# Linear attention and a gated expert layer on one core: the last 64 tokens' logits in full-width products, and their output rows in one store

## The chip, the cores and the metric

The kernel runs on one core of one Trainium2 chip. The metric is the device time of one execution in microseconds; the median of several executions is compared. TensorE (PE, with its weight loads PEld) multiplies matrices into PSUM; VectorE (DVE), ScalarE (ACT) and GpSimd (POOL) work element by element; SyncE (SP) issues most of the transfers. Transfers between the chip's memory and SBUF are moved by 16 DMA engines, whichever queue they were issued on. Each of the five engines takes its own instructions in order and waits on semaphores for the others.

## What is computed

Attention without a softmax, then a layer of eight experts of which each token uses one:

```
q_p, k_p = phi(q), phi(k)            # phi(x) = max(x, exp(x) - 1 for x <= 0) + 1
kv  = k_p^T v  per batch and head;   z = sum over the sequence of k_p
x   = (q_p kv) / (q_p . z + 1e-6)    # 8 batches, 576 tokens, 8 heads x 64 = 512 features
logits = x @ w_gate                  # 8 experts
fresh = argmax(logits); local = sigmoid(x @ w_local)
e     = fresh, if it is the first token or local < 0.5, else the expert of the token before
out   = softmax(logits)[e] * (relu(x @ w1[e]) @ w2[e])
```

q, k and v are (8, 8, 576, 64), w1 is (8, 512, 1024), w2 (8, 1024, 512), the output (8, 576, 512), all float32. If in a batch all tokens end with the expert of the first one, one pass with that expert's weights does for all of them. The kernel computes this case, counts tokens for which it doesn't hold, and runs a general version behind a branch (`tc.If(anybad > 0)`) only if there are any. In the runs here the branch is not taken.

## The kernel before

**Tokens.** A batch's 576 tokens lie as 64 rows of nine (`C` = 9): token 9p + c belongs to row p. Tokens with c = 1 to 8 form four chunks of 128 (`SM` = 512 of them), and those with c = 0 form a fifth chunk of 64, called the last one; the first token of the batch is in it. `NC` is 5, `PH` is 64.

**Stages of one batch.** SP loads k, q and v of two groups of four heads. ACT and DVE compute phi. PE multiplies k^T v (`kvs`, L299), transposes q (`q_main`, L310; `q_last`, L324), and multiplies q kv (`num_main`, L351; `num_last`, L370); DVE divides by the denominator (`divide`, L336 to L339). PE transposes x in bf16 (`x_main`, L385; `x_last`, L397), and DVE copies it from PSUM to the tile `xT`, [128, 4, 576]: 512 features as four blocks of 128 partitions, tokens along the free dimension. `x_main_out` (L390) copies two chunks of 128 tokens, `x_last_out` (L401) the 64 of the last chunk. Three `xT` tiles are in rotation.

**Logits.** `logits(b, cs)` multiplies chunks of `xT` by `wg`, the eight gate columns and the local one, into a PSUM tile of nine columns for each chunk (L412, L418). It is called twice for each batch: once for the last chunk alone, as early as it can be, because `pick` reads the first token's expert from it (its maximum, L429), which starts the load of that expert's weights on POOL's queue (L476, L478); and once for the other four chunks. The PSUM tile has 128 partitions. For the last chunk `logits` fills both halves: for each half d it runs four products with the same 64 tokens as the stationary operand (L412), so eight products of 64 columns. Later `gate_sub` and `gate_end` read all five chunks over 128 partitions.

**Experts and output.** `hidden` (L530) and `output` (L547, L551) multiply by w1 and w2; ACT evacuates them (L537, L561, L563). For the last chunk `output` computes columns 0 to 255 of the 64 tokens on the partitions 0 to 63 and columns 256 to 511 on the partitions 64 to 127, so that the tile `yl` is [128, 256]: partition 64h + p holds half h of the row of token 9p. `store` writes the four large chunks from `yo` (L570) and the last chunk from `yl` (L575) in two transfers, one for each half, from SP's queue. In the last batch the first of the two goes out on ACT's queue.

**Order.** The program is written out by a planner: `in_order` takes operations with an engine, an estimated length, a rank, what they need and which PSUM slot they take, and returns one order. The work is emitted in that order under `tc.manual_schedule()`, so each engine's instructions run in the order of the list. Two batches of attention run ahead of the experts (`LEAD` = 2).

**Fill products.** At the start PE has nothing to do while the first loads arrive. `work(n)` puts products of a tile of zeros ahead of some operations of batch 0 (`fills`, L741): 14 before `QL` (the first `q_last`), 8 before `K` (the first `kvs`), 15 in all before eight others. Each has 512 columns. `zero` is set by a memset at L167, `ones`, used as one column at the end in `total` (L588), at L184.

**End.** After the last store all engines load the counter `flag_i` (L749), branch over the general version (L751) and meet at the end of the program (L986).

Of the kernel before, what the change touches and what calls it, by code (L numbers as in the profile page):

```python
# [10 lines left out]
F32 = mybir.dt.float32  # L11
BF16 = mybir.dt.bfloat16
# [68 lines left out]
def kernel(  # L81
# [11 lines left out]
    nc = tc.nc  # L93
    P = 128
    B, H, S, Dh = q.shape
    D = H * Dh
    E = moe_w_gate.shape[1]
    F = moe_w1.shape[2]
    DK = D // P
    FK = F // P  # L100
    PH = P // 2


    C = S // PH
    NJ = 2

    NC = 5
    SM = (NC - 1) * P
# [8 lines left out]
    consts = ctx.enter_context(tc.tile_pool(name="consts", bufs=1))  # L117
# [3 lines left out]
    bad = keep.tile([P, B, NC], F32, name="bad")  # L121
# [3 lines left out]
    with ExitStack() as main:  # L125
# [37 lines left out]
                load(vraw[n % NV].rearrange("p g c d -> p g (c d)"), v, n)  # L163


        zero = consts.tile([P, 512], BF16, name="zero")
        nc.vector.memset(zero, 0.0)  # L167
        for n in range(NJ):
            load_q0(n)
# [10 lines left out]
            nc.sync.dma_start(out=wgf[:, :, E:E + 1],  # L180
                              in_=moe_w_local.rearrange("(ko ki) e -> ki ko e", ki=P))

        ones = consts.tile([P, P], F32, name="ones")
        nc.vector.memset(ones, 1.0)  # L184
        ident = consts.tile([P, P], F32, name="ident")
        make_identity(nc, ident)
# [6 lines left out]
        wg = consts.tile([P, DK, E + 1], BF16, name="wg")  # L193
# [7 lines left out]
        xtp = main.enter_context(tc.tile_pool(name="xtp", bufs=NX))  # L201
# [5 lines left out]
        ps_m = main.enter_context(tc.tile_pool(name="ps_m", bufs=2, space=PSUM))  # L207

        BK = 512

        def bank2(pool, name, tag, dt=F32):
            return pool.tile([P, 2, BK if dt == F32 else 2 * BK], dt, name=name, tag=tag)

        kv, qT, xb, xb4, xT, gate, hT, ex_ = {}, {}, {}, {}, {}, {}, {}, {}
# [68 lines left out]
        open_ = {}  # L283
# [49 lines left out]
        def divide(ps, m, dst):  # L333

            den = sm_.tile([P, 2, m], F32, name=f"den{m}")
            nc.vector.tensor_scalar(den, ps[:, :, :, Dh], 1e-6, None, Alu.add)  # L336
            rec = sm_.tile([P, 2, m], F32, name=f"rec{m}")
            nc.vector.reciprocal(rec, den)
            nc.vector.tensor_tensor(  # L339
                dst, ps[:, :, :, :Dh],  # L340
                rec.rearrange("p g (m o) -> p g m o", o=1).to_broadcast([P, 2, m, Dh]), op=Alu.mult)
# [32 lines left out]
        def num_last_out(a):  # L374
            ps = open_.pop(("NL", a))
            xb4[a] = xbp.tile([P, 2, P], BF16, name="xb4")
            divide(ps[:, :, :2 * W].rearrange("p g (m w) -> p g m w", w=W), 2,
                   xb4[a].rearrange("p g (t e) -> p g t e", t=2))
# [18 lines left out]
                nc.tensor.transpose(ps[:, 0, g * P:(g + 1) * P], xb4[a][:, g, :], identity=identb)  # L397

        def x_last_out(a):
            xT[a] = xtp.tile([P, DK, S], BF16, name="xT")  # L400
            nc.vector.tensor_copy(  # L401
                xT[a][:, :, SM:].rearrange("q (j g) p -> q g j p", g=2),
                open_.pop(("XL", a))[:, 0, :2 * P].rearrange("q (g j p) -> q g j p", g=2, j=2))

        rt, st = {}, {}

        def logits(b, cs):
            lps = open_["R", b, cs[0]] = bank2(ps_a, "lps", "a")[:, 0, :NC * (E + 1)].rearrange("p (c e) -> p c e", c=NC)
            if cs[-1] == NC - 1:
                for d in range(2):  # L410
                    for kk in range(DK):
                        nc.tensor.matmul(lps[d * PH:(d + 1) * PH, NC - 1, :],  # L412
                                         lhsT=xT[b][:, kk, SM:], rhs=wg[:, kk, :],
                                         start=(kk == 0), stop=(kk == DK - 1))
            for c in cs:
                if c < NC - 1:
                    for kk in range(DK):
                        nc.tensor.matmul(lps[:, c, :], lhsT=xT[b][:, kk, c * P:(c + 1) * P],  # L418
                                         rhs=wg[:, kk, :], start=(kk == 0), stop=(kk == DK - 1))

        def logits_out(b, cs):
            lps = open_.pop(("R", b, cs[0]))
            nc.vector.tensor_copy(lt_all[:, b, cs[0]:cs[-1] + 1], lps[:, cs[0]:cs[-1] + 1])

        def pick(b):

            m8 = sm_.tile([1, 8], F32, name="m8")
            i8 = sm_.tile([1, 8], U32, name="i8")
            nc.vector.max_with_indices(m8, i8, lt_all[0:1, b, NC - 1, :E])  # L429
            e0f = sm_.tile([1, 1], F32, name="e0f")  # L430
            nc.vector.tensor_copy(e0f, i8[:, 0:1])
            if b == 0:
                nc.vector.tensor_copy(tag[:, 0:1], e0f)
                rt[b] = (i8, e0f, None, None)
                return

            sc = sm_.tile([1, E], F32, name="sc8")
            nc.vector.scalar_tensor_tensor(sc, tag, e0f, age, Alu.is_equal, Alu.add)
            ms = sm_.tile([1, 8], F32, name="ms")
            si = gp.tile([1, 8], U32, name="si")  # L440
            nc.vector.max_with_indices(ms, si, sc)
            miss = sm_.tile([1, 1], I32, name="miss")
            nc.vector.tensor_scalar(miss, ms[:, 0:1], 1.0, None, Alu.is_lt)
            rt[b] = (i8, e0f, si, miss)
            st[b, "sc"] = (sc, ms)
# [119 lines left out]
        def store(b, i0, i1):  # L565
            o = out[b].rearrange("(p c) d -> p c d", c=C)
            ym, yl = yo[b]
            if i0 < NC - 1:
                for r in range(2):
                    nc.sync.dma_start(out=o[:, 1 + i0 + (NC - 1) * r:1 + i1 + (NC - 1) * r, :],  # L570
                                      in_=ym[r::2, i0:i1, :])
            else:
                for h in range(2):
                    eng = nc.scalar if b == B - 1 and h == 0 else nc.sync
                    eng.dma_start(out=o[:, 0, h * (D // 2):(h + 1) * (D // 2)],  # L575
                                  in_=yl[h * PH:(h + 1) * PH])

        def flags():

# [5 lines left out]

        def total():
            tot = open_["TOT"] = bank2(ps_a, "tot", "a")[0:1, 0, :B * NC]
            nc.tensor.matmul(tot, lhsT=ones[:, 0:1], rhs=bad.rearrange("p b c -> p (b c)"),  # L588
                             start=True, stop=True)

        def flag():
# [7 lines left out]
        def op(name, eng, length, rank, needs, fn, takes=None, gives=None):  # L599
            ops.append((name, eng, length, rank, [d for d in needs if d], takes, gives))  # L600
            run[name] = fn
# [7 lines left out]
        for a in range(B):  # L609
            at = (a - LEAD) * NU  # L610
            quick = a < LEAD
            for j in range(NJ):
# [3 lines left out]
                head = 60 * (a == 0)  # L616
# [59 lines left out]
               lambda a=a: num_last(a), takes="a")  # L676
            op(("DL", a), "DVE", 0.8, at - 3 - 2 * head, [("NL", a), a and ("XL", a - 1)],
               lambda a=a: num_last_out(a), gives=("NL", a))
            for h in range(2):
                cs = [NC - 1] if h == 0 else list(range(NC - 1))  # L680
                op(("X", a, h), "PE", 0.5, at + 6 + 4 * h - head, [("D", a, 0, h), ("D", a, 1, h)],
                   lambda a=a, h=h: x_main(a, h), takes="a")
                op(("XC", a, h), "DVE", 0.7, at + 1 + 3 * h - head, [("X", a, h)],
                   lambda a=a, h=h: x_main_out(a, h), gives=("X", a, h))
                op(("R", a, h), "PE", 0.2 + 0.3 * h, at + 4 + 7 * h - 2 * head * (1 - h),
                   [("WG",)] + ([("XC", a, 0), ("XC", a, 1)] if h else [("XLC", a)]), lambda a=a, cs=cs: logits(a, cs), takes="a")
                op(("RC", a, h), "DVE", 0.2, at - 3 + 8 * h - 2 * head * (1 - h), [("R", a, h)],
                   lambda a=a, cs=cs: logits_out(a, cs), gives=("R", a, h))
            op(("XL", a), "PE", 0.2, at + 3 - 2 * head, [("DL", a)], lambda a=a: x_last(a), takes="a")
            op(("XLC", a), "DVE", 0.3, at - 3 - 2 * head, [("XL", a), a >= NX and ("H", a - NX, FK - 1)], lambda a=a: x_last_out(a), gives=("XL", a))  # L690
            op(("PK", a), "DVE", 0.8, at - 3 - 2 * head, [("RC", a, 0), a and ("BK", a - 1)], lambda a=a: pick(a))
            op(("BK", a), "DVE", 0.65 if a else 0.02, at + 8, [("PK", a)], lambda a=a: book(a))
            for x in range(2):
                op(("W", a, x), "POOL", 1.2, at + x - head,
# [5 lines left out]
                    (("H", 0, 3) if x == 0 else ("O", 0, 1))],  # L700
                   lambda a=a, x=x: use(a, x))
            gr = at + NU
            op(("S1", a), "DVE", 0.6, gr, [("PK", a), ("RC", a, 0), ("RC", a, 1)],
               lambda a=a: gate_sub(a))
            op(("S2", a), "ACT", 0.25, gr, [("S1", a)], lambda a=a: gate_exp(a))
            op(("S3", a), "DVE", 1.4, gr + 3, [("S2", a)], lambda a=a: gate_end(a))
# [27 lines left out]
        order, begun, done = in_order(ops, {"a": 2, "m": 2, "ek": NK}, 0.2)  # L734

        with tc.manual_schedule():
            fill = bank2(ps_m, "fill", "m")[:, 0, :]

            def work(n):
                for _ in range(n):  # L740
                    nc.tensor.matmul(fill, lhsT=zero[:, :P], rhs=zero, start=True, stop=True)  # L741

            fills = {("QL", 0): 14, ("K", 0): 8, ("NL", 0): 2, ("XL", 0): 4, ("R", 0, 0): 2,
                     ("N", 0, 0, 1): 2, ("N", 0, 1, 0): 1, ("N", 0, 1, 1): 1, ("X", 0, 0): 1, ("X", 0, 1): 2}
            for name in order:
                work(fills.get(name, 0))
                run[name]()
# [243 lines left out]
```

## Time and profile before

| | us |
|---|---|
| median of three runs | 237.54 (235.86, 237.54, 241.7) |
| the profiled execution | 237.42 |
| its span in the trace | 235.3 |
| PE busy (share of the span) | 214.0 (91%) |
| ACT busy | 155.2 (66%) |
| DVE busy | 153.1 (65%) |
| the two calls of `logits`, products' busy time (L412; L418) | 2.4; 4.5 |

The profile is that of one execution. Busy times overlap, and the chain of waits follows the work that ended last back from its end: it says where a shorter step would shorten the whole. In rows of groups the columns are line, engine, operation, output <- input with shapes, count, then the busy time in us and the mean of one in ns, and the engine's idle time ahead with what ended it. In a timeline they are start, length, engine (a q behind it is the engine's instruction queue) and operation. A row of a stretch of time has its length, each engine's busy time (instructions), TensorE's granted clock as a share of full speed, the DMA engines' busy share and GB/s. The granted clock over the whole span is 0.985.

### The profile page before, as it was taken

Reading aid. Unit: us, or ns where it says so; the run is one execution under the profiler, and the core shown is the slowest. Engines: PE = TensorE matmul, PEld = TensorE weight load, DVE = VectorE, ACT = ScalarE, POOL = GpSimd, SP = SyncE. Lnnn points to the kernel's source line nnn. Section 1 sums busy time; section 2 is a strip of 40 time slices with the busy share of each in tenths; the row PEclk is TensorE's granted clock in tenths of the full one; section 3 lists DMA queues with packets and bytes.
Section 4 is the critical chain, followed back from the end, with each engine's and each line's share of the span. In section 5 each row is a group of like instructions: output and inputs, shape, how many; then the busy total and the mean of one; then the engine's idle time right before and its main releaser. Section 6 shows DMA issues by size and latency. Waiting matters only on the chain.

```text
span 235.3 us, 8595 instructions
## 1 busy us (share of the span) xinstructions
PE 214.0 (91%) x3701; PEld 150.8 (64%) x3719; DVE 153.1 (65%) x428; ACT 155.2 (66%) x226; POOL 11.4 (5%) x40
## 2 busy tenths in 40 slices
PE   7786999799999989997789999999999999999970
PEld 2454787566777667864578756885687657647530
DVE  2877985999899969988838899378543665202000
ACT  3699549996899997679657895583335525546540
POOL 3002000000000002000000010110000011000000
PEclk9999999999999999999979999999999999999996
DMA  6999999947973876999677539960050069915041
GB/s 215 381 349 332 202 313 398 374 128 243 367 290 102 278 235 214 204 284 295 204 274 252 181 96 227 219 102 3 3 205 3 0 100 277 168 19 203 3 157 52
DMA packets 23614, 46.78 MB, mean 199 GB/s; under 512 B 2818, under 2 KB 7938, under 8 KB 22674
## 3 DMA queue, kind: packets, MB, share of 16 engines
q1 hardware_dynamic: 16914, 37.58, 45.0%
q0 software_dynamic: 6304, 8.45, 21.9%
q8 instruction: 31, 0.51, 0.9%
q10 hardware_dynamic: 352, 0.13, 0.2%
q14 instruction: 13, 0.11, 0.2%
HBM read 61.88 MB, written 9.44 MB: 303 GB/s over the span
## 4 chain that ended last, share of the span: by engine, by line
PE 70%; DMA 12%; DVE 7%; ACT 4%; issue 3%; SPq 0%; DVEq 0%; ACTq 0%; POOLq 0%
PE hps L530 24%; PE yps L547 21%; PE kvps L299 7%; DMA qraw<-in_q_dram 5%; PE nps L351 5%; PE tq L310 5%; DMA kraw<-in_k_dram 4%; PE tx L385 3%; PE yps L551 3%; DMA q<-in_q_dram 2%; DVE xb L339 2%; ACT ek L243 1%; PE lps L418 1%; ACT qT L316 1%; DVE fq L278 1%
## 5 line engine op out<-in xcount | busy, mean ns | idle before, releaser
L530 PE MATMUL hps<-xT,w1cur 128*128 128x288 bf16 x512 | 70.2, 288 | 1.6 <-ACT yo L561 1.6
L547 PE MATMUL yps<-w2cur,hT 128*128 128x512 bf16 x241 | 57.6, 379 | 1.7 <-issue 1.2
L537 ACT ACTIVATE hT<-hps 128x576 bf16<-128x576 f32 x64 | 41.3, 660 | 25.7 <-PE hps L530 25.7
L530 PEld LDWEIGHTS <-w1cur 128*128 128x128 bf16 x512 | 48.1, 98 | 14.6 <-issue 2.6
L561 ACT ACTIVATE yo<-yps,pr 128x512 f32<-128x512 f32 x32 | 21.9, 685 | 28.0 <-PE yps L547 27.9
L547 PEld LDWEIGHTS <-hT 128*128 128x128 bf16 x256 | 23.6, 98 | 25.7 <-issue 0.5
L351 PE MATMUL nps<-kv,qT 64*64 64x65 f32 x1024 | 21.3, 222 | 4.4 <-ACT qT L316 2.4
L351 PEld LDWEIGHTS nps<-kv,qT 64*64 64x64 f32 x1024 | 17.7, 134 | 9.9 <-issue 3.6
L339 DVE TENSOR_TENSOR xb<-nps,rec 128x512 bf16<-128x512 f32 x32 | 22.1, 692 | 1.1
L278 DVE SCALAR_TENSOR_TENSOR fq<-fq,qraw 128x576 f32<-128x576 f32 (+1 forms) x32 | 22.6, 742 | 0.1
L243 ACT ACTIVATE fq<-qraw 128x1152 f32<-128x1152 f32 (+1 forms) x16 | 18.5, 1157 | 5.9 <-DMA qraw<-in_q_dram 5.8
L299 PEld LDWEIGHTS kvps<-vone,kraw 64*64 64x64 f32 x1152 | 19.1, 139 | 3.6 <-issue 1.7
L299 PE MATMUL kvps<-vone,kraw 64*64 64x65 f32 x1152 | 21.2, 225 | 0.2 <-PE tx L385 0.2
L243 ACT ACTIVATE ek<-kraw 128x1152 f32<-128x1152 f32 x16 | 18.5, 1159 | 3.5 <-DMA kraw<-in_k_dram 2.6
L316 ACT COPY qT<-tq 128x512 f32<-128x512 f32 x32 | 18.3, 634 | 1.4 <-PE tq L310 1.4
L271 DVE SCALAR_TENSOR_TENSOR kraw<-ek,kraw 128x1152 f32<-128x1152 f32 x14 | 18.9, 1348 | 0.0
L249 ACT ACTIVATE qraw<-qraw 128x1152 f32<-128x1152 f32 (+1 forms) x16 | 18.4, 1153 | 0.3
L310 PE MATMUL tq<-ident,fq 128*128 128x128 f32 x128 | 16.8, 274 | 1.6 <-DVE fq L278 0.9
L249 ACT ACTIVATE kraw<-kraw 128x1152 f32<-128x1152 f32 x14 | 16.3, 1167 | 0.2
L310 PEld LDWEIGHTS tq<-ident,fq 128*128 128x128 f32 x128 | 14.4, 141 | 3.1 <-issue 1.4
L492 DVE COPY w1cur<-w1s 128x4096 bf16 x7 | 8.6, 1226 | 8.4 <-PE hps L530 7.3
L304 DVE COPY kv<-kvps 128x130 f32<-128x130 f32 x16 | 4.6, 289 | 13.9 <-PE kvps L299 13.9
(93 smaller groups left out, 189.3 us busy)
## 6 DMA issues: line engine op xcount, KB each, us to landing
kraw<-in_k_dram SPq DMA_DIRECT2D x16, 576.0 KB, 7.2
vraw<-in_v_dram SPq DMA_DIRECT2D x16, 576.0 KB, 7.5
qraw<-in_q_dram SPq DMA_DIRECT2D x14, 576.0 KB, 6.5
w1s<-in_moe_w_dram POOLq DMA_DIRECT2D x7, 1024.0 KB, 10.2
w2s<-in_moe_w_dram POOLq DMA_DIRECT2D x7, 1024.0 KB, 15.4
out_dram<-yo SPq DMA_DIRECT2D x14, 512.0 KB, 4.6
qraw<-in_q_dram SPq DMA_DIRECT2D x2, 512.0 KB, 8.8
w1cur<-in_moe_w_dram POOLq DMA_DIRECT2D x1, 1024.0 KB
```

Of the source, the lines that this page charges most:

```text
L243: nc.scalar.activation(e[:, :, c0:c1, :], raw_, Act.Exp)
L249: nc.scalar.activation(raw_, raw_, Act.Relu)
L278: nc.vector.scalar_tensor_tensor(e[:, g], e[:, g], 1.0, r[:, g], Alu.min, Alu.add)
L299: nc.tensor.matmul(ps[g * PH:(g + 1) * PH, t, :W], lhsT=f[h, g, c, :], rhs=vo[h, g, c, :], start=(c == 0), stop=(c == C - 1))
L310: nc.tensor.transpose(ps[:, r, i * P:(i + 1) * P], ex_[n, "q"][:, 1 + i + (NC - 1) * r, :, :], identity=ident)
L316: nc.scalar.copy(qT[n][:, :, :SM].rearrange("q t (i p r) -> q r t i p", i=NC - 1, r=2)[:, r], ps[:, r, :].rearrange("q (i t p) -> q t i p" ...
L339: nc.vector.tensor_tensor(dst, ps[:, :, :, :Dh], rec.rearrange("p g (m o) -> p g m o", o=1).to_broadcast([P, 2, m, Dh]), op=Alu.mult)
L351: nc.tensor.matmul(ps[o * PH:(o + 1) * PH, g, (il * 2 + t) * W:(il * 2 + t + 1) * W], lhsT=qT[n][g * PH:(g + 1) * PH, t, i * P + o * PH:i ...
L530: nc.tensor.matmul(ps[:, u, :HS], lhsT=w1b[:, kk, m * P:(m + 1) * P], rhs=xT[b][:, kk, u * HS:(u + 1) * HS], start=(kk == 0), stop=(kk == ...
L537: nc.scalar.activation(hT[b][:, m, :].rearrange("p (u s) -> p u s", u=2), open_.pop(("H", b, m))[:, :, :HS], Act.Relu)
L547: nc.tensor.matmul(ps[:, 0, :], lhsT=hT[b][:, m, i * P:(i + 1) * P], rhs=w2b[:, m, :], start=(m == 0), stop=(m == FK - 1))
L561: nc.scalar.activation(ym[:, i, :], ps[:, 0, :], Act.Copy, scale=pr[:, i:i + 1])
```

## The change

Three things change.

1. `xT` gets 64 more columns. `x_last_out` writes the last 64 tokens twice, side by side, from the same 64 columns in PSUM, read twice with a step of 0. `logits` then takes the last chunk like any other: four products with 128 stationary columns in place of eight with 64.
2. `store` writes `yl` in one transfer. Its target in memory is written out by hand as three dimensions: 2 halves of 256 columns, 64 tokens 9 x 512 elements apart, 256 elements in a row. It goes out on SP's queue, in the last batch on ACT's.
3. The fill products have 384 columns for 512, and 18 and 10 of them stand before `QL` and `K` in place of 14 and 8. `zero` has 384 columns, and `ones` has one column in place of 128.

The lines about `apart` add a switch that is set to the way it was before; `R` of the four large chunks now also names `XLC` among its needs. The order of instructions on each engine is the same as before, apart from those that are added or left out.

```diff
-        zero = consts.tile([P, 512], BF16, name="zero")
+        zero = consts.tile([P, 384], BF16, name="zero")
...
-        ones = consts.tile([P, P], F32, name="ones")
+        ones = consts.tile([P, 1], F32, name="ones")
...
         def x_last_out(a):
-            xT[a] = xtp.tile([P, DK, S], BF16, name="xT")
+            xT[a] = xtp.tile([P, DK, S + PH], BF16, name="xT")
             nc.vector.tensor_copy(
-                xT[a][:, :, SM:].rearrange("q (j g) p -> q g j p", g=2),
-                open_.pop(("XL", a))[:, 0, :2 * P].rearrange("q (g j p) -> q g j p", g=2, j=2))
+                xT[a][:, :, SM:].rearrange("q (j g) (o p) -> q g j o p", g=2, o=2),
+                open_.pop(("XL", a))[:, 0, :2 * P].rearrange(
+                    "q (g j o p) -> q g j o p", g=2, j=2, o=1).to_broadcast([P, 2, 2, 2, PH]))
...
         def logits(b, cs):
-            if cs[-1] == NC - 1:
-                for d in range(2):
-                    for kk in range(DK):
-                        nc.tensor.matmul(lps[d * PH:(d + 1) * PH, NC - 1, :],
-                                         lhsT=xT[b][:, kk, SM:], rhs=wg[:, kk, :],
-                                         start=(kk == 0), stop=(kk == DK - 1))
             for c in cs:
-                if c < NC - 1:
-                    for kk in range(DK):
-                        nc.tensor.matmul(lps[:, c, :], lhsT=xT[b][:, kk, c * P:(c + 1) * P],
-                                         rhs=wg[:, kk, :], start=(kk == 0), stop=(kk == DK - 1))
+                for kk in range(DK):
+                    nc.tensor.matmul(lps[:, c, :], lhsT=xT[b][:, kk, c * P:(c + 1) * P],
+                                     rhs=wg[:, kk, :], start=(kk == 0), stop=(kk == DK - 1))
...
         def store(b, i0, i1):
...
-                for h in range(2):
-                    eng = nc.scalar if b == B - 1 and h == 0 else nc.sync
-                    eng.dma_start(out=o[:, 0, h * (D // 2):(h + 1) * (D // 2)],
-                                  in_=yl[h * PH:(h + 1) * PH])
+                eng = nc.scalar if b == B - 1 else nc.sync
+                eng.dma_start(out=bass.AP(out.tensor, b * S * D, [[D // 2, 2], [C * D, PH], [1, D // 2]]),
+                              in_=yl)
...
-            fill = bank2(ps_m, "fill", "m")[:, 0, :]
+            fill = bank2(ps_m, "fill", "m")[:, 0, :384]
...
-            fills = {("QL", 0): 14, ("K", 0): 8, ("NL", 0): 2, ("XL", 0): 4, ("R", 0, 0): 2,
+            fills = {("QL", 0): 18, ("K", 0): 10, ("NL", 0): 2, ("XL", 0): 4, ("R", 0, 0): 2,
```

More of the change, by code (lines that the diff above doesn't have):

```diff
@@ L587, in total @@
             tot = open_["TOT"] = bank2(ps_a, "tot", "a")[0:1, 0, :B * NC]
-            nc.tensor.matmul(tot, lhsT=ones[:, 0:1], rhs=bad.rearrange("p b c -> p (b c)"),
+            nc.tensor.matmul(tot, lhsT=ones, rhs=bad.rearrange("p b c -> p (b c)"),
                              start=True, stop=True)
@@ L678 @@
                lambda a=a: num_last_out(a), gives=("NL", a))
+            apart = True
             for h in range(2):
-                cs = [NC - 1] if h == 0 else list(range(NC - 1))
+                cs = [NC - 1] if h == 0 else list(range(NC - apart))
                 op(("X", a, h), "PE", 0.5, at + 6 + 4 * h - head, [("D", a, 0, h), ("D", a, 1, h)],
@@ L684 @@
                    lambda a=a, h=h: x_main_out(a, h), gives=("X", a, h))
-                op(("R", a, h), "PE", 0.2 + 0.3 * h, at + 4 + 7 * h - 2 * head * (1 - h),
-                   [("WG",)] + ([("XC", a, 0), ("XC", a, 1)] if h else [("XLC", a)]), lambda a=a, cs=cs: logits(a, cs), takes="a")
-                op(("RC", a, h), "DVE", 0.2, at - 3 + 8 * h - 2 * head * (1 - h), [("R", a, h)],
+                if not (h or apart):
+                    continue
+                up = 2 * head * (1 - h) if apart else 4
+                op(("R", a, h), "PE", 0.2 + 0.3 * h, at + 4 + 7 * h - up,
+                   [("WG",), ("XLC", a)] + [("XC", a, g) for g in range(2) if h],
+                   lambda a=a, cs=cs: logits(a, cs), takes="a")
+                op(("RC", a, h), "DVE", 0.2, at - 3 + 8 * h - up, [("R", a, h)],
                    lambda a=a, cs=cs: logits_out(a, cs), gives=("R", a, h))
@@ L690 @@
             op(("XLC", a), "DVE", 0.3, at - 3 - 2 * head, [("XL", a), a >= NX and ("H", a - NX, FK - 1)], lambda a=a: x_last_out(a), gives=("XL", a))
-            op(("PK", a), "DVE", 0.8, at - 3 - 2 * head, [("RC", a, 0), a and ("BK", a - 1)], lambda a=a: pick(a))
+            op(("PK", a), "DVE", 0.8, at - 3 - 2 * head, [("RC", a, int(not apart)), a and ("BK", a - 1)], lambda a=a: pick(a))
             op(("BK", a), "DVE", 0.65 if a else 0.02, at + 8, [("PK", a)], lambda a=a: book(a))
@@ L702 @@
             gr = at + NU
-            op(("S1", a), "DVE", 0.6, gr, [("PK", a), ("RC", a, 0), ("RC", a, 1)],
+            op(("S1", a), "DVE", 0.6, gr, [("PK", a), ("RC", a, 1)],
                lambda a=a: gate_sub(a))
```

## The prediction

> **What bounds the kernel now.** I read the page's table of busy time and its row of chain shares first, then the chain of waits in order of time.
>
> ```profile
> PE 214.0 (91%) x3701; PEld 150.8 (64%) x3719; DVE 153.1 (65%) x428; ACT 155.2 (66%) x226; POOL 11.4 (5%) x40
> ...
> PE 70%; DMA 12%; DVE 7%; ACT 4%; issue 3%; SPq 0%; DVEq 0%; ACTq 0%; POOLq 0%
> ```
>
> TensorE (PE) is busy 214.0 of 235.3 us and holds 70% of the chain; transfers hold 12%. So a saving counts where the chain runs through PE, and a later transfer costs time only where somebody waits for it. Columns of the chain: start, length, work.
>
> ```profile
> 24.26 0.32 PE fill L741
> ...
> 25.04 0.43 PE fill L741 x2
> ...
> 40.44 0.27 PE lps L412 x8
> ...
> 63.99 0.28 DVE xT L401
> ...
> 75.11 0.38 PE lps L418 x16
> ...
> 94.19 0.49 PE lps L418 x16
> ...
> 101.58 12.47 DMA qraw<-in_q_dram
> ...
> 134.00 0.23 PE lps L412 x8
> ...
> 159.25 0.23 PE lps L412 x8
> ...
> 184.49 0.23 PE lps L412 x8
> ...
> 228.10 0.47 ACT yl L563
> ```
>
> The eight half-width logit products (L412) are on the chain four times in eight batches, the copy that the change widens (L401) once, the fill products three times; the one large transfer wait after the start is a load of q that lands at 114.05. What comes behind the last `yl` at 228.57 is not in the chain and is read below.
>
> The profiled execution took 237.42 us, 2.1 more than its span; the median of three runs is 237.54 (235.86 to 241.7). The sum goes against 237.42; 2% of it, about what a measurement of this kernel can tell from no change, is 4.75 us.
>
> **Logits.** Eight half products cost 0.23 to 0.27 us where they are on the chain. Sixteen full-width ones cost 0.38 to 0.49, so 0.024 to 0.031 each, and four of them 0.10 to 0.12. The step loses 0.13 to 0.15 us. Four places on the chain make 0.54; all eight batches would make 1.1, none 0. I take -0.5.
>
> **The copy.** It writes 512 elements a partition where it wrote 256, from the same 256 in PSUM.
>
> ```profile
> L339 DVE TENSOR_TENSOR xb<-nps,rec 128x512 bf16<-128x512 f32 x32 | 22.1, 692 | 1.1
> ...
> L390 DVE COPY xT<-tx 128x1024 bf16<-128x1024 bf16 x16 | 10.9, 683 | 2.1 <-PE tx L385 1.9
> ...
> L401 DVE COPY xT<-txl 128x256 bf16<-128x256 bf16 x8 | 2.3, 286 | 2.1 <-PE txl L397 2.1
> ```
>
> The nearest rows are two copies of the same kind: (683-286)/768 = 0.52 ns an element, so 256 more cost 0.13 us. The other bound is the 512-element operation from float PSUM, 0.69 us: 0.41 more. I take the copy's own row, as only the repeated read differs. In late batches it has cover:
>
> ```profile
> 158.35 0.28 DVE L401 COPY xT<-txl 128x256 bf16<-128x256 bf16 x1
> ...
> 159.18 0.30 PE L412 MATMUL lps<-wg,xT 128*64 128x9 bf16 x8
> ```
>
> It ends at 158.63, and PE comes to the logits at 159.18, behind a hidden-layer step. So it costs about 0.13 on the chain once (63.99); with that cover gone everywhere and the dear price, 8 x 0.41 = 3.3. I take +0.2. The slots, the wider `xT` rows and the order of instructions on each engine are otherwise as they were.
>
> **Fills.** A fill product has 384 columns for 512; 37 become 43, in total 16,512 columns for 18,944. The three on the chain shrink by a quarter of 0.75, 0.19 us; the products behind the second pair wait for VectorE as well, so I take -0.1 (0 to -0.3, with the shorter run ahead of the first `kvps`). The two smaller memsets are ahead of any wait for data: nothing.
>
> **The store of `yl`.** One transfer takes the place of two in each batch. Its bytes, rows of 1 KB and their number are the same, but its target is written as 2 x 64 x 256, where each half was 64 x 256. What the leading 2 does is the doubtful point, and the packet counts bear on it (queue, packets, MB, share; then the issues):
>
> ```profile
> q1 hardware_dynamic: 16914, 37.58, 45.0%
> ...
> q10 hardware_dynamic: 352, 0.13, 0.2%
> ...
> kraw<-in_k_dram SPq DMA_DIRECT2D x16, 576.0 KB, 7.2
> ...
> q<-in_q_dram ACTq DMA_DIRECT2D x1, 64.0 KB, 4.4
> ...
> out_dram<-yl ACTq DMA_DIRECT2D x1, 64.0 KB, 3.1
> ...
> there<-w1cur SPq DMA_DIRECT2D x1, 0.0 KB
> ```
>
> q10 is ScalarE's queue: 64 KB of q in runs of 256 B are 256 packets, its `yl` half is 64 rows, and 352-256-64 leaves 32, so 16 for each transfer: I read them as one completion from each of 16 engines. On q1, SyncE's, the eleven rows of its issues, the first and last of which stand here, hold 86 transfers; their runs, counted the same way (one packet for each contiguous run, 2304 B for most loads), come to 15,553, and 1,361 are left: 85 x 16 and one. Transfers whose outermost dimension is 64 or 128 finish on 16 engines, and `there`, a single element, on one. So the engines follow the outermost dimension, and with 2 there I expect two engines. No transfer of this trace has a 2, so that is an inference.
>
> The Trainium skill, "DMA: Bandwidth & Descriptors", section "Rules for kernel authors", says the same and speaks against this change: the slowest dimension that is not 1 sets how many engines work, and fewer than 16 there confine the whole DMA. By it the sum is the one with two engines; were the store spread, it would be the first rival's.
>
> The price of a row comes from the end of the kernel (packets of the queue, 228.5 to 235.3 us):
>
> ```profile
> q10 hardware_dynamic: 80, 0.07, 3.7%
> ```
>
> 3.7% of 16 engines over 6.8 us is 4.0 us for 64 rows, 0.06 us each. Spread, 128 rows hold each engine for 8 x 0.06 = 0.5 us; on two engines 64 x 0.06 = 3.9. Whatever is queued behind that store on those two is up to 3.4 us late, and a load has landed only when all its shares have. The next limit is where someone waits.
>
> *In the middle.* The only stretch with loads behind a `yl` store and waits for them is 88 to 120 us:
>
> ```profile
> 87.84 1.94 SPq L575 DMA_DIRECT2D out_dram<-yl  x2
> ...
> 91.82 0.76 POOL L478 DMA_DIRECT2D w1s<-in_moe_w_dram  x1 [22.60 <-DVE rec L338]
> ...
> 94.25 0.39 SPq L143 DMA_DIRECT2D kraw<-in_k_dram  x1
> ```
> ```profile
> 92.00:96.00 4.00, 4.00 (x114) 3.58 (x112) 3.86 (x13) 2.69 (x4) 1.47 (x2) 1.00 0.72 91
> 104.00:120.00 16.00, 12.36 (x180) 8.01 (x180) 12.10 (x35) 11.47 (x15) 0.44 (x4) 0.97 0.86 255
> 118.00:124.00 6.00, 5.45 (x108) 4.67 (x108) 2.03 (x12) 3.00 (x6) 0.22 (x2) 0.72 0.69 253
> ```
> ```profile
> ACT fq L243 <- DMA qraw<-in_q_dram: 4.4, 2, 2.6
> DVE w1cur L492 <- DMA w1s<-in_moe_w_dram: 0.6, 1, 0.6
> ```
>
> Behind the store come the expert weights and, 6 us later, the next k. Between 92 and 96 the engines are busy 0.72 of the time (the figure before the last in the row), so 1.1 us of 4 could take up the backlog on average, and the two lists share the engine. ScalarE already waits 4.4 us here for q, VectorE 0.6 for weights; PE is idle 3.6 of the 16 us from 104 to 120. So of 3.4 us between none and all comes through; I take +0.8, the nearer to none for the 1.1 and for the 6 us before the next k. In the first burst (60 us) ScalarE shows no wait for q, so loads have some room: +0.3, bounds 0 and 3.4. From 137 on no load is left, and stores there delay nobody. SyncE's queue is relieved of one issue in each batch (0.5 to 1.4 us), ahead of its loads; I count that at nothing, as the loads are held by the engines, not by the issue.
>
> *At the end.*
>
> ```profile
> 228.61 0.55 ACTq L575 DMA_DIRECT2D out_dram<-yl  x1
> 229.02 1.23 SPq L575 DMA_DIRECT2D out_dram<-yl  x1
> ```
> ```profile
> L751 SPq EVENT_SEMAPHORE  x8: 17/17/17, 231.6 to 232.2; - x8
> ...
> L751 PEldq COMPARE_BRANCH  x1: 3678/3678/3678, 227.7 to 227.7; - x1
> ```
> ```profile
> L986 SPq DRAIN  x3: 7/7/13, 233.0 to 234.7; - x3
> ...
> L986 PEldq DRAIN  x2: 8/8/8, 234.4 to 234.7; - x2
> ```
>
> SyncE has seen the last store land at 232.2 and is ready at 233.0, but all engines then wait for PE, whose branch out of the loop takes 3.7 us and which is ready at 234.4. So one issue less on SyncE gains nothing, and a store that lands later has 1.4 us of cover. On two engines: ScalarE's half landed 3.1 us after its issue, at 231.7, with 4 rows an engine; 60 more at 0.06 make 235.3, SyncE is ready 0.8 later, and that is 1.7 past PE. This is the upper bound, since the 3.1 hold a wait behind the `yo` stores just before, which not every engine need have had; the lower is 0. I take +0.3.
>
> **Sum:** 237.42 - 0.5 (logits) - 0.1 (fills) + 0.2 (copy) + 0.8 (middle) + 0.3 (first burst) + 0.3 (end) = 238.4.
>
> **Rivals.** *The store is spread over 16 engines after all*: the delays go, 237.42-0.5-0.1+0.1 (the copy's one place) = 236.9. For it: nothing in the trace has tried a leading 2.
> *The backlog comes through whole* (slower): at 88 us the two engines don't catch up, and q lands at 117.5 for 114.05: +3.4. PE's idle time of 3.6 then doubles, and the granted clock, 0.72 on the mean from 118 to 124, stays low for another such stretch: 0.28 x 6 = +1.7. With the sum's other terms (-0.5-0.1+0.2+0.3+0.3) that makes 242.7. It decides if less than about 0.5 us of the backlog is drained by 101. Against it: the 0.72.
> *The copy's repeated read drops to the dear price*: +0.41 in the four batches up to 106 us, with cover only later: 238.4 + 1.4 = 239.8; the logits' saving is then paid back by the copy that it needs.
> *The shorter SyncE queue moves the loads ahead* (faster): the wait for q goes with PE's 3.6 us and half of the clock's 1.7: 236.9-4.5 = 232.4. Against it: the engines, 0.86 busy over those 16 us, not the issues, hold the loads.
>
> **Numbers.** Forecast 0.50, spread store 0.27, backlog whole 0.12, dear copy 0.06, loads ahead 0.05. The forecast's own range is 236.9 to 240.5 (middle term 0 to 2.4, the others as bounded). The range 235.6 to 241.0 takes in the spread store and the dear copy, with the logits' full 1.1 and the fills' 0.3 below (236.1) and half a microsecond for the spread of the runs; it leaves out the backlog whole and the loads ahead. Faster by over 2%: 0.05; slower: 0.12 and a little of the forecast's tail, 0.13; within: 0.82.
>
> **What would show it.** Two engines: q10 has 256+128+16+2 = 402 packets (416 if spread), q1 16,624 (16,722 if spread), and SyncE's eight semaphore waits end near 234. The logit step: four products of 128x9 in about 0.11 us. The copy: near 416 ns. The middle: ScalarE's wait for q between 90 and 125 us grows from 4.4. I am wrong if q10 shows 416, if the copy takes 0.69, or if PE's idle time from 104 to 120 shrinks.

## The result, and the profile after

| | before | changed |
|---|---|---|
| median of 22 runs each, us | 237.2 (235.59 to 242.1) | 238.24 (236.38 to 240.33) |
| span of the profiled execution, us | 235.3 | 236.1 |
| mean granted clock over the span | 0.985 | 0.987 |
| from the end of the last `yl` to the end of the span, us | 6.7 | 7.0 |

The ratio of the times is 1.0059, with a 95% interval of 1.003 to 1.0087: about 1.4 us slower, well inside the 2% called no change, but not zero. The ratio leaves out runs over 1.5% above the fastest of their kernel, so it is not the quotient of the medians (1.004). The changed kernel's line numbers differ by up to six: the logits are L413, `hidden` L525, the evacuation of `yl` L558, its store L569.

The page of the changed kernel (busy table, two queues, shares of the chain):

```profile
PE 213.6 (90%) x3693; PEld 151.3 (64%) x3693; DVE 153.7 (65%) x428; ACT 154.8 (66%) x226; POOL 10.9 (5%) x40
...
q1 hardware_dynamic: 16624, 37.51, 45.2%
...
q10 hardware_dynamic: 402, 0.20, 0.3%
...
PE 68%; DMA 12%; DVE 8%; ACT 6%; issue 3%; SPq 0%; DVEq 0%; ACTq 0%; POOLq 0%
```

The packets are the forecast's two-engine counts exactly: 402 and 16,624. PE's share of the chain fell by two points and ACT's rose by two. The chain of waits of the changed kernel (start, length, work) says where:

```profile
64.03 0.42 DVE xT L402
...
101.22 13.19 DMA qraw<-in_q_dram
...
133.48 1.14 ACT qT L316 x2
...
158.71 1.14 ACT qT L316 x2
...
183.91 1.14 ACT qT L316 x2
...
228.55 0.47 ACT yl L558
```

At 134, 159 and 184 us, where the chain ran through the last chunk's logits before, it now runs through ScalarE's copy of q^T. The changed kernel's timeline at the second of these places (start, length, engine, line and operation):

```profile
158.71 1.13 ACT L316 COPY qT<-tq 128x512 f32<-128x512 f32 x2 [0.22 <-PE tq L310]
158.86 0.41 DVE L402 COPY xT<-txl 128x512 bf16<-128x512 bf16 x1
...
159.60 0.25 PE L413 MATMUL lps<-wg,xT 128*128 128x9 bf16 x4
...
159.89 0.70 PE L351 MATMUL nps<-kv,qT 64*64 64x65 f32 x32
```

and the kernel before's, the row ahead of those that stand in the prediction and the one behind them:

```profile
158.20 1.14 ACT L316 COPY qT<-tq 128x512 f32<-128x512 f32 x2 [0.22 <-PE tq L310]
...
159.42 0.70 PE L351 MATMUL nps<-kv,qT 64*64 64x65 f32 x32
```

`nps` needs `qT`. Before, the copies ended at 159.34 and `nps` began 0.08 us behind, at 159.42; now they end at 159.84 and it begins 0.05 us behind, at 159.89. The shorter logits no longer hold `nps`, the copies do, and only some 0.03 us was there to be gained.

The end of the changed kernel: the last issue in the timeline, PE's instructions at the branch (L751) and the two engines' first arrival at the end of the program (L986; the columns are shortest, median and longest duration in ns, then first and last start).

```profile
229.05 1.12 ACTq L569 DMA_DIRECT2D out_dram<-yl  x1
```
```profile
L751 SPq EVENT_SEMAPHORE  x8: 17/17/17, 231.0 to 234.4; - x8
...
L751 PEldq COMPARE_BRANCH  x1: 3542/3542/3542, 228.1 to 228.1; - x1
...
L751 PEldq EVENT_SEMAPHORE  x1: 51/51/51, 231.7 to 231.7; - x1
```
```profile
L986 SPq DRAIN  x3: 7/7/13, 235.2 to 235.5; - x3
...
L986 PEldq DRAIN  x2: 8/8/8, 231.9 to 235.6; - x2
```

Here the roles have changed over. SyncE sees the store land at 234.4 and is ready at 235.2, the last of all; PE is ready at 231.9, where it was last at 234.4 before. PE's branch takes as long as it did. What has gone is what came behind it, in the kernel before at the same place:

```profile
L751 PEldq EVENT_SEMAPHORE  x1: 51/51/51, 231.4 to 231.4; - x1
```

There 3.0 us pass from that instruction (231.4) to PE's arrival (234.4); in the changed kernel 0.2. Nothing in the diff touches PE at that place. That, and the price of the store, is what the experiments are about.

### The profile page after: what moved, and what is told of

Its sections match the earlier page's. It is cut to its first block, busy times and chain, and to the rows that moved or that the text cites. A ratio compares the mean times of both kernels' runs of the same rounds, so it can differ in the third digit from the quotient of the medians.

```text
span 236.1 us, 8551 instructions
## 1 busy us (share of the span) xinstructions
PE 213.6 (90%) x3693; PEld 151.3 (64%) x3693; DVE 153.7 (65%) x428; ACT 154.8 (66%) x226; POOL 10.9 (5%) x40
## 3 DMA queue, kind: packets, MB, share of 16 engines
q1 hardware_dynamic: 16624, 37.51, 45.2%
## 4 chain that ended last, share of the span: by engine, by line
PE 68%; DMA 12%; DVE 8%; ACT 6%; issue 3%; SPq 0%; DVEq 0%; ACTq 0%; POOLq 0%
PE hps L525 22%; PE yps L542 21%; PE kvps L299 7%; DMA qraw<-in_q_dram 6%; PE nps L351 5%; PE tq L310 5%; DMA kraw<-in_k_dram 4%; PE tx L385 3%; ACT qT L316 3%; PE yps L546 3%; DVE xb L339 2%; DMA q<-in_q_dram 2%; ACT ek L243 1%; PE lps L413 1%; DVE fq L278 1%
## 5 line engine op out<-in xcount | busy, mean ns | idle before, releaser
L525 PE MATMUL hps<-xT,w1cur 128*128 128x288 bf16 x512 | 70.3, 288 | 1.6 <-ACT yo L556 1.6
L542 PE MATMUL yps<-w2cur,hT 128*128 128x512 bf16 x256 | 59.5, 379 | 0.0
L525 PEld LDWEIGHTS <-w1cur 128*128 128x128 bf16 x512 | 48.2, 98 | 14.8 <-issue 2.6
L487 DVE COPY w2cur<-w2s 128x4096 bf16 x7 | 8.6, 1224 | 8.4 <-PE yps L546 8.2
```

Of the source, the lines that this page charges most:

```text
L525: nc.tensor.matmul(ps[:, u, :HS], lhsT=w1b[:, kk, m * P:(m + 1) * P], rhs=xT[b][:, kk, u * HS:(u + 1) * HS], start=(kk == 0), stop=(kk == ...
L542: nc.tensor.matmul(ps[:, 0, :], lhsT=hT[b][:, m, i * P:(i + 1) * P], rhs=w2b[:, m, :], start=(m == 0), stop=(m == FK - 1))
```

## The experiments

The theory: the store on two engines costs time in the middle, by late loads, and at the end; the end's cost is hidden as long as PE returns late. The rivals: the store costs nothing and the difference lies in the logits, the copy or the fills; PE's early return comes from the shorter work ahead of the branch, or from where the code lies that PE jumps to. Each ratio is against the kernel before on the same chip, with its 95% interval.

**The two halves put back into the changed kernel**, three times, and the single store put into the kernel before:

```diff
-                eng = nc.scalar if b == B - 1 else nc.sync
-                eng.dma_start(out=bass.AP(out.tensor, b * S * D, [[D // 2, 2], [C * D, PH], [1, D // 2]]),
-                              in_=yl)
+                for h in range(2):
+                    eng = nc.scalar if b == B - 1 and h == 0 else nc.sync
+                    eng.dma_start(out=o[:, 0, h * (D // 2):(h + 1) * (D // 2)],
+                                  in_=yl[h * PH:(h + 1) * PH])
```

> The changed kernel, but the yl store as two transfers of 64 rows again, in every batch. Theory A (the loss is the store that runs on two DMA engines): all 16 engines again, 352 packets on ScalarE's queue; the wait for q near 114 us is back to some 2.6 us; at the end SyncE is ready some 4.4 us after the last ACT, and as PE returned at 231.9 in the changed kernel, it is SyncE that sets the end: about 1.4 us under the kernel before, ratio 0.994 (0.991 to 0.998). Theory B (the loss is the wider copy, or the logits don't save): the ratio stays near 1.006.

> The changed kernel with two halves once more, for the comparison within one chip: 0.991, as before (0.986 to 0.995), tail 5.7 us; the clock in the stretch from 118 to 124 us may drop or not, as nothing in the edit decides it.

> Two halves in every batch, once more, as the version that should beat both kernels on the same chip: 0.993 (0.989 to 0.997), 1.0% or more under the changed kernel, tail 5.3 to 5.7 us.

Measured: 0.9906 (0.9859 to 0.9953), 0.9959 (0.9915 to 1.0002) and 0.9892 (0.9837 to 0.9947). Weighted by their precision they make 0.992 ± 0.003: without the single store the change is a gain of 0.8%, 1.8 us. The end of the first of them, by its chain and its arrivals:

```profile
226.53 0.47 ACT yl L558
```
```profile
L987 SPq DRAIN  x3: 7/7/13, 231.8 to 232.1; - x3
...
L987 PEldq DRAIN  x2: 8/8/8, 230.4 to 232.2; - x2
```

From the end of the last `yl` (227.0) SyncE takes 4.8 us and PE 3.4; the span ends at 232.7, 5.7 behind, and this stretch is called the tail. PE is as early as in the changed kernel, and SyncE 1.4 us earlier.

The reverse of the diff, in the kernel before:

> The kernel before, with only the yl store made one transfer. Theory A: 402 packets on ScalarE's queue, the q load near 114 us lands about 0.7 us later after its issue, and SyncE is ready some 6.2 us after the last ACT, later than PE's return at 234.4: +0.4 to +1.4 us, ratio 1.002 to 1.006. Theory B: ratio 1.000.

Measured: 1.0012 (0.9962 to 1.0063). PE returns late here, 6.3 us behind the last `yl`, as in the kernel before (5.8), and SyncE is ready at 6.6: nearly all of the late store lies beside PE's return, the tail grows by 0.8 us (7.5 for 6.7), and the step as a whole can't be told from none.

**The single store in the last batch only, and in all but the last.** Both start from the changed kernel and use the two halves elsewhere; the first one's edit is shown, the second has `b < B - 1` in its place:

```diff
+                if b == B - 1:
                     eng = nc.scalar if b == B - 1 else nc.sync
                     eng.dma_start(out=bass.AP(out.tensor, b * S * D, [[D // 2, 2], [C * D, PH], [1, D // 2]]),
                                   in_=yl)
+                else:
+                    for h in range(2):
...
```

> The changed kernel with one yl transfer in the last batch only, two in the seven others. If the store on two engines costs at the end what the tails of the profiles say (7.0 us from the end of the last ACT to the span's end in the changed kernel, 5.7 with two halves), this is 1.3 us over the kernel with two halves: ratio 0.996 (0.992 to 1.000), and SyncE's ready point some 6.2 us after the last ACT. If the end costs nothing, 0.991.

> One yl transfer in the last batch only, once more, for the difference to the changed kernel on one chip: 1.004 (0.999 to 1.008), tail 7.1 us.

> The changed kernel with one yl transfer in the first seven batches, two in the last. Tail 5.7 us as with two halves. If the backlog of the two engines in the middle makes the rest of the difference between the changed kernel (1.006) and two halves (0.991), the ratio is about 1.000 (0.996 to 1.003); if the middle costs nothing, 0.991.

Measured: single in the last batch 1.004 (1.0 to 1.0081) and 1.0006 (0.9963 to 1.0048), together 1.002 ± 0.003; single in the other seven 0.9959 (0.9914 to 1.0005), the same as the second run of the two halves, measured beside it. The first of these lies above what was expected (0.992 to 1.000). The arrivals, first with the single store last (last `yl` ends at 230.8), then with it in the others (232.1):

```profile
L992 SPq DRAIN  x3: 7/7/13, 237.1 to 237.4; - x3
...
L992 PEldq DRAIN  x2: 8/8/8, 233.6 to 237.5; - x2
```
```profile
L992 SPq DRAIN  x3: 7/7/13, 236.9 to 237.3; - x3
...
L992 PEldq DRAIN  x2: 8/8/8, 235.2 to 237.3; - x2
```

SyncE is ready 6.3 us behind `yl` with the single store at the end, 4.8 without it. PE is early in both.

**The changed kernel once more**, beside two of these:

> The changed kernel once more, beside the others on one chip: 1.006 (1.000 to 1.010), tail 7.0 us. Against the version with one transfer in the last batch only (1.004 before) it holds the price of the other seven stores in one transfer: 0.4% by my sum, 0 if the middle costs nothing.

Measured: 1.0064 (1.0027 to 1.0101); with the first comparison 1.006 ± 0.002. The four kernels give each price twice. The end: single last against two halves 1.002 - 0.992, changed against single others 1.006 - 0.996, both 1.0%, with an error of ±0.3 in their mean, 2.4 us. The middle: single others against two halves 0.996 - 0.992, changed against single last 1.006 - 1.002, both 0.4% ± 0.3, 0.9 us. The end is settled. The middle shows only when the pairs are pooled: pairs measured beside each other give 0.0 and 0.6%. The single store in the kernel before speaks against it: its tail alone adds 0.8 us (0.3%), and 0.9 us more in the middle would make 1.007, just above its interval (0.9962 to 1.0063).

**The fills alone**, in the kernel before: the smaller `zero`, `ones` and fill products, and nothing else.

```diff
-            fills = {("QL", 0): 14, ("K", 0): 8, ("NL", 0): 2, ...
+            fills = {("QL", 0): 18, ("K", 0): 10, ("NL", 0): 2, ...
```

> The kernel before, with only the fill products changed (384 columns, 18 and 10 of them) and the two smaller constant tiles. Both theories: within 0.3 us up to the last ACT; 0.998 to 1.001. PE's program is 12 instructions longer; if PE's late return at the end depends on where the code behind the branch lies, it may return 2.5 us earlier, and then SyncE sets the end, 1.4 us sooner: 0.994.

Measured: 0.9955 (0.9894 to 1.0015), which can't be told from none. But PE is ready 3.1 us behind the last `yl`, and the tail is 5.4 us. The early return comes with the fills too, which run 200 us earlier.

**Code that never runs.** `general`, the version behind the branch, gets 30 products more in the kernel before; nothing that is executed changes. And the changed kernel with two halves gets 26 products there (`range(26)`). A product is two PE instructions, a weight load and a matmul. The changed kernel has 32 products fewer in `logits` and 6 more fills, so 52 PE instructions fewer, and 26 products bring its PE program back to the length of the kernel before.

```diff
+            pad = two("gpad")
+            for i in range(30):
+                nc.tensor.matmul(pad[:, 0, :P], lhsT=identb, rhs=identb, start=True, stop=True)
```

> The kernel before, with 60 PE instructions more in the general version, which is never entered, so that only the place of the code behind the branch moves. Theory A, second part (PE's return at 234.4 is a fetch of instructions across a boundary, and it sets the end of the kernel before): PE is ready near 232, SyncE's 233.0 sets the end, -1.4 us, ratio 0.994 (0.992 to 0.997). Rival (PE returns late for another reason, or its return doesn't matter): ratio 1.000.

> The changed kernel with two halves, and 52 PE instructions more in the general version, which is never entered, so that the program is as long as in the kernel before. Theory A, second part: PE returns some 6.3 us after its last product again, past SyncE, and the tail is 6.7 in place of 5.7 us: ratio 0.995 (0.991 to 0.999). Rival (PE's return has nothing to do with the place): 0.991 and a tail of 5.7.

Measured: the kernel before with 30 products that never run is faster, 0.9939 (0.9893 to 0.9985); the two halves with 26 are slower, 1.005 (1.0008 to 1.0092), against 0.9959 for the same kernel without them, measured beside it. That is more than was expected (0.991 to 0.999), but the direction and the tail (7.3 us for 6.7) are as forecast. The arrivals of the first (last `yl` at 229.3) and of the second (228.5):

```profile
L989 SPq DRAIN  x3: 7/7/13, 234.0 to 234.3; - x3
...
L989 PEldq DRAIN  x2: 8/8/8, 232.6 to 234.4; - x2
```
```profile
L990 SPq DRAIN  x3: 7/7/13, 232.9 to 235.2; - x3
...
L990 PEldq DRAIN  x2: 8/8/8, 234.9 to 235.3; - x2
```

In the first PE is ready 3.3 us behind `yl` and SyncE is last; in the second PE is ready at 6.4, back where it was before. All runs read in this way (us behind the end of the last `yl`; the tail ends with the span):

| kernel | PE instructions against before | PE ready | SyncE ready | tail |
|---|---|---|---|---|
| before | 0 | 5.8 | 4.4 | 6.7 |
| before, single store | 0 | 6.3 | 6.6 | 7.5 |
| two halves, 26 products | 0 | 6.4 | 4.4 | 7.3 |
| before, fills alone | +12 | 3.1 | 4.5 | 5.4 |
| before, 30 products | +60 | 3.3 | 4.7 | 5.6 |
| two halves (three runs) | -52 | 3.0 to 3.4 | 4.4 to 4.8 | 5.3 to 5.7 |
| two halves, `yo` store cut (below) | -52 | 3.1 | 5.0 | 5.8 |
| single in others | -52 | 3.1 | 4.8 | 5.7 |
| single in last (two runs) | -52 | 2.8, 3.3 | 6.3, 6.2 | 7.2, 7.1 |
| changed (two runs) | -52 | 2.9, 3.1 | 6.2 | 7.0, 7.1 |

The tail is the later of the two and 0.8 to 0.9 us. Over all the kernels PE's return goes with the length of its program, late with one length and early with all the others, and SyncE's with the last store alone. The shorter work ahead of the branch can't be the cause: the 30 products change none of it.

**A large backlog in the middle.** To see what a late load costs there, the kernel with two halves cuts the first `yo` store of batch 1 into rows 0 to 61 and 62 to 63, the first of which has 62 for its outermost dimension:

```diff
-                    nc.sync.dma_start(out=o[:, ...], in_=ym[r::2, i0:i1, :])
+                    for p0, p1 in ((0, 62), (62, 64)) if b == 1 and r == 0 else ((0, 64),):
+                        nc.sync.dma_start(out=o[p0:p1, ...], in_=ym[r + 2 * p0:2 * p1:2, i0:i1, :])
```

> The changed kernel with two yl halves, and in batch 1 the first of the two large yo stores cut into 62 and 2 rows, so that (if the engines follow a divisor of the outermost dimension) 62 rows of 8 KB run on two engines, some 11 us on each: about three times the excess of a yl store in one transfer, at the same place, ahead of the loads that end near 114 us. If a backlog on two engines there comes through to the waiting ScalarE, q lands 3 to 10 us later after its issue (12.6 us with spread stores) and the ratio is 1.005 to 1.03; if it is drained before the loads need those engines, 0.993 as with two halves.

Measured: 1.0164 (1.0107 to 1.0222), where the two halves without it, measured beside it, had 0.9892: 2.7%, 6.5 us. The queue, the load in the chain, and waits between 80 and 130 us (total, times, longest):

```profile
q1 hardware_dynamic: 16902, 37.58, 44.9%
```
```profile
104.49 18.76 DMA qraw<-in_q_dram
```
```profile
DVE w1cur L487 <- DMA w1s<-in_moe_w_dram: 7.4, 1, 7.4
...
ACT ek L243 <- DMA kraw<-in_k_dram: 5.4, 1, 5.4
ACT fq L243 <- DMA qraw<-in_q_dram: 4.1, 2, 2.2
```

Against 16,914 the queue has 12 packets fewer: 16 completions have become 4, which fits 2 for the 62 rows and 2 for the 2 rows: 62 shares only the factor 2 with 16. The load of q takes 18.8 us, 12.6 in the kernel without the cut, and VectorE waits 7.4 us for weights. So a long backlog on two engines does come through to the end here.

## Why the prediction held, and where its steps did not

The time came out at 238.24 for 238.4, and that it came so near is luck in part. The changed kernel is 1.4 us slower by the ratio, for the 1.0 that was forecast, and three things in the sum were wrong, not all with one sign: the logits gave almost nothing of their 0.5, the store at the end cost 2.4 us where 0.3 stood, and PE's early return, which the sum did not have, is worth 1.2 (with two halves the tail is 5.5 us on the mean, for 6.7 in the kernel before).

**Two engines for the leading 2: right**, from packet counts alone; 402 and 16,624 came as forecast, and the rival of the spread store falls. The Trainium skill, "DMA: Bandwidth & Descriptors", section "Rules for kernel authors", has the slowest dimension that is not 1 set the number of engines; the packet counts for the 2 and the 62 agree with it (two completions each).

**The copy: right.** These are two groups of the changed kernel (mean in ns behind the busy time):

```profile
L402 DVE COPY xT<-txl 128x512 bf16<-128x512 bf16 x8 | 3.3, 418 | 1.6 <-PE txl L397 1.6
...
L741 PE MATMUL fill<-zero 128*128 128x384 bf16 x43 | 10.2, 373 | 1.3 <-DVE ones L184 1.3
```

418 ns for the 416 of the copy's own row, so the repeated read keeps its rate, and the dear copy falls. The copy is on the chain once, at 64.03, as forecast.

**The fills, -0.1:** a product takes 373 ns (second row above), and none is on the chain of the changed kernel any more, but nothing of their own could be told apart; what the fills alone gain (0.4%, unresolved) goes with PE's early return, 1.3 us of tail.

**The logits, -0.5: the price was right, the overlap was wrong.** At 40 us, where PE goes on to a hidden-layer step without a wait, PE's own saving is whole (changed kernel, then the kernel before):

```profile
40.47 0.25 PE L413 MATMUL lps<-wg,xT 128*128 128x9 bf16 x4
40.57 0.65 PE L525 MATMUL hps<-xT,w1cur 128*128 128x288 bf16 x4
```
```profile
40.37 0.30 PE L412 MATMUL lps<-wg,xT 128*64 128x9 bf16 x8
40.60 0.67 PE L530 MATMUL hps<-xT,w1cur 128*128 128x288 bf16 x4
```

From the start of the logits to that of the next step 0.10 us pass now and 0.23 before, near the 0.11 that was forecast. (The lengths of 0.25 and 0.30 reach into the next step.) The step that failed is to count this at all four places on the chain. Here the chain goes on to VectorE's copy of the logits, which starts 0.28 us behind them now and 0.36 before; at the other three the next step waits for the copies of `qT` too, which leave some 0.03 us to be gained. From the end of batch 3's `yl` to that of batch 7's the kernels with old logits take 82.82 to 82.83 us, all with the new ones 82.76 to 82.78: 0.06 us, where 0.13 at two places (159 and 184) would make 0.27. The prediction asked where its other edits were covered and not what stood right beside this one, though the row of `qT` was in the trace.

**The middle and the first burst, +0.8 and +0.3: the size fits, but it is not settled.** The pooled pairs make 0.9 ± 0.7 us, and the kernel before with the single store speaks for less. The sign that was named, ScalarE's wait for q, went from 4.4 to

```profile
ACT fq L243 <- DMA qraw<-in_q_dram: 5.1, 2, 3.4
...
DVE w1cur L487 <- DMA w1s<-in_moe_w_dram: 0.7, 1, 0.7
```

(the changed kernel, 85 to 125 us), but one trace can't show so small a cost. Take all runs but the one with the cut `yo` store. The load of q takes 12.5 to 13.6 us in the nine with two halves in batch 1, and 13.2 to 15.0 in the four with the single store; ScalarE's wait is 4.3 to 5.2 and 4.6 to 5.6; from the end of batch 1's `yl` to that of batch 2's 32.1 to 33.4 and 32.8 to 34.6 us pass. The load and the stretch are both 1.0 us longer on the mean, but they overlap. So part of the backlog probably comes through, and not the whole 3.4; the 6.5 us of the cut `yo` store show what a longer one costs there. PE's idle time from 104 to 120 us, a sign of being wrong if it shrank, went from 3.6 to 4.2. Loads ahead by the shorter queue are not seen: the load is issued at 101.22 for 101.58 and lands later, at 114.41.

**The end, +0.3: the step that failed.** "All engines then wait for PE" was right for the kernel before: the 30 products that never run take 0.6% off it. What was wrong is "a store that lands later has 1.4 us of cover": it took PE's 234.4 for a property of the branch (over the general version; it is no loop). It is one of the program's length, and the change itself shortens the program. Without that cover the store is the end. The price of the late store was within the upper bound: SyncE's wait ends 5.4 us behind the last `yl`, 3.6 before, so 1.8 later for at most 3.6. The DMA view from 228.5 us to the end of the changed kernel gives the price of a row again:

```profile
q10 hardware_dynamic: 130, 0.13, 3.7%
```

3.7% of 16 engines over 11.5 us (this window runs past the span, to 240) is 6.8 us for 128 rows, 0.053 each, 3.4 us on each of the two. The issue on ScalarE also takes longer, 1.12 us for 0.55.

**The sum as it was:** PE's early return and the rest of the edits -1.8 (two halves against before), the store at the end +2.4, in the middle +0.9, together +1.5, for a measured 1.4. This closes because the prices are differences of the same measurements; it is no test of them. The tails show 1.2 of the 1.8 and 1.6 of the 2.4 (7.1 for 5.5 on the mean); the rest is no more than about the error of 0.7 and has no cause shown. The best kernel here is the changed one with the two halves: 0.992 of the kernel before, 1.4% below the changed one.

Why PE returns 3 us late with one length is only argued. The runs show that code which is never executed decides it, and that 52 instructions fewer, 12 or 60 more all do away with it. The profiles list a queue of instruction transfers, and in the kernel before one of its 16 KB transfers starts 3.5 us behind the last `yl`, ahead of PE's arrival at 5.8, in the changed one 3.3 behind, after PE's arrival at 2.9. All runs have one there, 0.7 us (once 1.2) behind the end of PE's branch; in the three late kernels PE arrives 1.3 to 1.5 us behind its end, in the others ahead of its start. That fits a target of the branch whose next instructions lie in the block before or behind a boundary. Whose transfer it is the trace doesn't say, and other lengths were not tried.

## What to carry to other kernels

Count the outermost dimension of a transfer's target before two stores are merged into one: here a leading 2 left two engines of sixteen, and as the last stores of the program two transfers of 64 rows made the kernel 1% faster than one of 128. Cover at the end of a program is only as good as the reason for it: ask what makes the last engine late, and whether the change touches that, even through code that never runs. Before a step on the chain is given a gain, look at what else the next step waits for, and how far behind that ends.

## What the hardware showed that was not expected

Never-executed code moves the time by 0.6 to 0.9% in either direction (30 products more: 0.9939; 26 more: 1.005 for 0.9959), through 3 us of PE's return from one branch.

All but one of the profiled executions had TensorE at half clock for 3.4 or 6.8 us before the end, from 8 to 9, 111 to 113 or 118 to 121 us on, three of them at two of these places, and the place changed between runs of the same kernel. Here is the kernel with two halves (third run), then the changed one; the third figure from the end is the granted clock:

```profile
8.00:12.00 4.00, 3.38 (x21) 1.74 (x25) 3.23 (x5) 2.67 (x5) 0.00 (x0) 0.67 1.05 380
...
118.00:122.00 4.00, 1.86 (x23) 1.53 (x23) 2.05 (x3) 4.00 (x5) 0.22 (x2) 1.00 0.53 148
```
```profile
8.00:12.00 4.00, 3.58 (x105) 2.67 (x109) 3.33 (x5) 2.63 (x5) 0.00 (x0) 1.00 1.06 380
...
118.00:122.00 4.00, 3.10 (x88) 2.87 (x91) 1.33 (x5) 3.05 (x6) 0.22 (x2) 0.81 0.63 256
```

The first run with two halves had none: its stretch from batch 2's `yl` to batch 3's took 24.4 us for 25.7 to 26.0 in kernels with one of 3.4 us there, so one costs about 1.4 us, as much as the whole effect of the change. Runs with one at 8 to 9 us end batch 0 at 62.1 to 62.7 us, the others at 59.1 to 61.5. One span against another says little here; the tail behind the last `yl` and the stretch from batch 3 to batch 7 repeat to 0.4 and 0.02 us.
